# One multiply moved to ScalarE and one group of transposes moved behind two matmul groups, in a recurrent-attention and SwiGLU kernel

## The chip, the core and the metric

The kernel runs on one core of one Trainium2 chip. The metric is the device time of one execution in microseconds (us), lower is better. The core has five engines with instruction queues of their own: TensorE (PE in the profile; its weight loads are shown as PEld), VectorE (DVE), ScalarE (ACT), GpSimd (POOL) and SyncE (SP), which here issues most of the DMAs. Each queue runs in its own order, and engines wait for each other by semaphores.

## The reference

Two stages. The first is a linear recurrence per batch and head, with a state of 48 x 48, a decay w per key column and a bonus u for the current token. The second is a normalised SwiGLU network over its output.

```python
r, k, v, w: (4, 8, 768, 48)   u: (8, 48)
for t in range(S):
    cur = einsum('bhd,bhe->bhde', u * k[t], v[t])
    y[t] = einsum('bhd,bhde->bhe', r[t], state + cur)
    state = w[t][..., None] * state + einsum('bhd,bhe->bhde', k[t], v[t])
x = y as (3072, 384)
xn = x / sqrt(mean(x * x) + 1e-6) * rms_g
g = xn @ w_gate                       # (384, 1536)
out = (g * sigmoid(g) * (xn @ w_val)) @ w_out
```

## The kernel before

**Tiling.** The 768 tokens are cut into six superblocks n of 128 tokens. A superblock has four units n.j, one for each batch j: 128 tokens on the partitions and 384 columns (8 heads of 48). The recurrence is computed by chunks: the logarithms of w are summed up along the tokens by a matmul with a triangle of ones (cs_mm, L394 to L419), r is multiplied by the exponential of that sum and k by that of its negative (r_mul, L454; k_mul, L460). Then r and k are transposed, the scores of each head are computed (q_mm, L494), masked, and multiplied with v (y_mm, L541); older tokens come in through the state (st_mm, st_new). The bonus is added as a column by token (bonus_mul, bonus_sum, bonus_v). k_mul is done by VectorE in superblocks 0 and 1 and by GpSimd in the others.

**Transposes of r and k.** In superblocks 0 and 1 they are matmuls with an identity, eight for a unit: four of r, then four of k (rk_pe, L483), into one bank of PSUM, which ScalarE copies out (rk_tr, L492). From superblock 2 on they are DMAs.

**The network.** x of a unit is scaled by its root mean square on ScalarE (xn_mul, L584) and transposed into x^T, a tile xnt of 128 partitions x 3 groups c x 512 tokens of the superblock. In superblocks 0 to 3 TensorE does it (xn_pe), and VectorE multiplies by rms_g while it copies out (xn_out). In superblocks 4 and 5 four DMA transposes do it (xn_tr, L589), and then three instructions n.c multiply the groups c of x^T by rms_g in place (xn_gain, L611, each 128 x 512). Then come twelve column groups f: gate_mm and val_mm (L622, three matmuls each, one for each group c in the order 0, 1, 2), silu on ScalarE (L635, shown under the helper's line L234), h_mul on VectorE (L640). After all twelve, o_mm (L654) multiplies by w_out, twelve matmuls for each batch, o_out copies and out_dma stores.

**Order.** The order of every queue is written out by hand in the string ORDER: a list of steps "function.n.j", issued one after the other. An engine's queue is the part of this list that concerns the engine. Work of neighbouring superblocks is mixed: while the network of superblock n runs, the recurrence of n + 1 is computed. Steps "warm" are idle matmuls at the start.

**Banks.** PSUM is dealt out in three rings: "a" of two banks (ps_au, ps_av: gate results and sums), "b" of two (ps_bu, ps_bv: value results and sums) and "q" of four (ps_qu, ps_qv, ps_qx, ps_qz: all the rest). A step takes the bank of its ring that has been free the longest in the order of the list (psum, L221), so moving a step can change banks. In this change no step gets another bank or follows another user in it. Of interest below: val_mm.0.0 and then val_mm.0.3 use ps_bu, gate_mm.0.0 and gate_mm.0.2 use ps_au, gate_mm.0.3 and gate_mm.0.1 use ps_av, and gate_mm.4.0 and gate_mm.4.3 use ps_av.

**Tables.** ScalarE computes exponentials and logarithms under one function table and silu under another; `act` loads the other table when it changes (L232). Copies with a scale go past `act` and ask for no table.

The pieces of the order around the two edits, as they were:

```python
... exp_k.1.2 rk_tr.1.0 k_mul.1.3 gate_mm.0.0
rk_pe.1.1 val_mm.0.2 st_new.0.1 gate_mm.0.3 bonus_sum.1.0 silu.0.0 load_gv.1.1 val_mm.0.0 gate_mm.0.2 silu.0.3 silu.0.2
bonus_sum.1.1 rk_tr.1.1 h_mul.0.0 h_mul.0.2 r_mul.1.3 gate_mm.0.1 val_mm.0.3 gate_mm.0.9 ...
...
exp_r.5.2 cs_mm.5.0 o_mm.3.3 cs_add.5.0 exp_r.5.0 exp_k.5.2 out_dma.2.1 exp_k.5.0 bonus_v.5.3 r_mul.5.2 out_dma.3.2
r_mul.5.0 cs_mm.5.3 bonus_mul.5.2 o_mm.3.0 cs_add.5.3 load_v.5.2 k_mul.5.1 exp_k.5.3 xn_gain.4.1 xn_gain.4.0
bonus_mul.5.1 xn_gain.4.2 exp_r.5.3 r_mul.5.3 gate_mm.4.0 rk_tr.5.1 val_mm.4.1 silu.4.0 k_mul.5.0 gate_mm.4.1 ...
```

Of the kernel before, what the change touches and what calls it, by code (L numbers as in the profile page):

```python
# [11 lines left out]
AF = mybir.ActivationFunctionType  # L12
# [28 lines left out]
x_rstd.0.2 st_new.0.0 warm.35.0 r_mul.1.1 warm.11.0 cs_mm.1.3 x_sq.0.3 warm.28.0 xn_pe.0.0 xn_out.0.1 xn_out.0.0  # L41
warm.0.0 st_new.0.3 xn_mul.0.2 x_rstd.0.3 exp_k.1.3 xn_mul.0.3 xn_pe.0.2 cs_mm.1.2 xn_out.0.2 xn_pe.0.3 xn_out.0.3
st_mm.0.2 rk_pe.1.0 st_mm.0.1 k_mul.1.1 exp_r.1.3 exp_r.1.2 st_new.0.2 exp_k.1.2 rk_tr.1.0 k_mul.1.3 gate_mm.0.0
rk_pe.1.1 val_mm.0.2 st_new.0.1 gate_mm.0.3 bonus_sum.1.0 silu.0.0 load_gv.1.1 val_mm.0.0 gate_mm.0.2 silu.0.3 silu.0.2
bonus_sum.1.1 rk_tr.1.1 h_mul.0.0 h_mul.0.2 r_mul.1.3 gate_mm.0.1 val_mm.0.3 gate_mm.0.9 silu.0.1 bonus_mul.1.3
val_mm.0.1 h_mul.0.3 silu.0.9 gate_mm.0.6 q_mm.1.0 bonus_sum.1.3 silu.0.6 gate_mm.0.7 q_copy_o.1.1 q_copy_o.1.0
q_mask_o.1.0 q_mask_o.1.1 gate_mm.0.5 rk_pe.1.3 bonus_v.1.0 h_mul.0.1 silu.0.7 val_mm.0.7 load_r.2.2 q_mask_e.1.0
# [56 lines left out]
st_mm.4.2 h_mul.3.5 val_mm.3.11 silu.3.11 bonus_mul.5.0 x_add.4.3 ln.5.1 x_sq.4.2 st_mm.4.3 h_mul.3.11 cs_mm.5.1  # L104
x_sq.4.3 x_rstd.4.2 xn_mul.4.2 cs_add.5.1 load_r.5.1 ln.5.3 xn_tr.4.0 o_mm.3.2 x_rstd.4.3 o_out.3.2 xn_tr.4.1 xn_tr.4.2
exp_r.5.1 xn_mul.4.3 ln.5.2 o_mm.3.1 ln.5.0 cs_mm.5.2 exp_k.5.1 r_mul.5.1 xn_tr.4.3 st_new.4.3 cs_add.5.2 out_dma.2.3
exp_r.5.2 cs_mm.5.0 o_mm.3.3 cs_add.5.0 exp_r.5.0 exp_k.5.2 out_dma.2.1 exp_k.5.0 bonus_v.5.3 r_mul.5.2 out_dma.3.2
r_mul.5.0 cs_mm.5.3 bonus_mul.5.2 o_mm.3.0 cs_add.5.3 load_v.5.2 k_mul.5.1 exp_k.5.3 xn_gain.4.1 xn_gain.4.0
bonus_mul.5.1 xn_gain.4.2 exp_r.5.3 r_mul.5.3 gate_mm.4.0 rk_tr.5.1 val_mm.4.1 silu.4.0 k_mul.5.0 gate_mm.4.1 rk_tr.5.0
k_mul.5.3 val_mm.4.0 k_mul.5.2 bonus_sum.5.0 silu.4.1 st_new.4.2 cast_v.5.2 cast_v.5.3 bonus_sum.5.1 gate_mm.4.3  # L110
o_out.3.1 gate_mm.4.2 h_mul.4.1 load_v.5.0 o_out.3.3 bonus_sum.5.2 silu.4.3 o_out.3.0 silu.4.2 val_mm.4.2 h_mul.4.2
# [20 lines left out]
def kernel(  # L132
# [13 lines left out]
    nc = tc.nc  # L146
# [7 lines left out]
    KC = DM // 128  # L154
# [3 lines left out]
    TS = SB * L  # L158
# [15 lines left out]
    def sel(s):  # L174
        return {(int(x[0]), int(x[1])) for x in s.split()}
# [10 lines left out]
    RK_PE = sel("00 01 02 03 10 11 12 13")  # L186
    RK_DVE = sel("")
    GAIN_POOL = sel("")
    RPAIR = ()
    ODD_DVE = sel("00 01 02 03")  # L190
    RSTD_ACT = sel("00 01 02 03")
# [4 lines left out]
    def banks_of(fn, n, j):  # L196
        if fn == "q_mm":
            return [(x, n, c) for c in ((j, j + 1) if (n, j) in Q_PAIR else (j,)) for x in ("qe", "qo")]
        found = {
            "cs_mm": ("cs_r",) if n in ONE_SUM else ("cs_r", "cs_k"), "cs_add": ("cs_k", "cs_r"),  # L200
            "exp_r": ("cs_r",), "exp_k": ("cs_k",),
            "w_tot": () if (n, j) in EXPR_SB else ("cs_r",), "r_mul": () if (n, j) in EXPR_SB else ("cs_r",),
            "k_mul": () if (n, j) in EXPK_SB else ("cs_k",),
            "rk_pe": ("tr",), "rk_tr": ("tr",) if (n, j) in RK_PE else (),
            "q_mask_e": ("qe",), "q_copy_o": ("qo",), "q_mask_o": ("qo",) if (n, j) in ODD_DVE else (),
            "st_mm": ("st",), "st_new": ("st",), "y_mm": ("y",), "x_add": ("y",), "x_pe": ("y",),
            "x_sq": ("y",) if (n, j) in X_PE else (), "xn_mul": ("y",) if (n, j) in X_PE else (),
            "xn_pe": ("xt",), "xn_out": ("xt",), "gate_mm": ("g",), "silu": ("g",),
            "val_mm": ("v",), "h_mul": ("v",), "o_mm": ("o",), "o_out": ("o",), "warm": ("warm",),
        }  # L210
        return [(x, n, j) for x in found.get(fn, ())]

# [2 lines left out]
    for i, step in enumerate(steps):  # L215
        for key in banks_of(*step):
            last_use[key] = i
# [3 lines left out]
    def psum(ring, key, shape, dtype=FP32):  # L221
        slots = rings[ring]
        k = min((x for x in range(len(slots)) if slots[x][0] < at[0]), key=lambda x: slots[x])
        taken[0] += 1
        slots[k] = [last_use.get(key, -1), taken[0]]
        return psP.tile(shape, dtype, name="ps_" + ring + "uvxz"[k])
# [46 lines left out]
    gT = small.tile([128, KC], FP32)  # L273
# [9 lines left out]
    for i in range(EARLY):  # L283
# [6 lines left out]
        out=mask_lt, in_=mask_lt, compare_op=ALU.is_ge, fill=1.0,  # L290
# [26 lines left out]
        out=mw, in_=mw, compare_op=ALU.is_ge, fill=1.0,  # L317
# [24 lines left out]
    wg_sb = [persist.tile([128, KC, (b - a) * 128], BF16, name="wg_sb%d" % a) for a, b in zip(GV, GV[1:])]  # L342
    wv_sb = [persist.tile([128, KC, (b - a) * 128], BF16, name="wv_sb%d" % a) for a, b in zip(GV, GV[1:])]
# [21 lines left out]
    xnt, ht = {}, {}  # L365
    bank = {}
# [196 lines left out]
    def x_sq(n, j):  # L563
        c = j % 2 if n in RPAIR else 0
        if (n, j) not in rstd:
            rstd[n, j] = small.tile([128, 2, 2], FP32, name="rstd", bufs=4)
            if n in RPAIR:
                rstd[n, j - j % 2] = rstd[n, j - j % 2 + 1] = rstd[n, j]
        nc.scalar.activation(out=junk, in_=xb[n, j], func=AF.Square, accum_out=rstd[n, j][:, 0, c:c + 1])

    def x_rstd(n, j):
        w = 2 if n in RPAIR else 1
        ss, rs = rstd[n, j][:, 0, 0:w], rstd[n, j][:, 1, 0:w]
        if (n, j) in RSTD_ACT:
            act(LN_EXP, out=ss, in_=ss, func=AF.Ln, scale=1.0 / DM, bias=eps_col)
            act(LN_EXP, out=rs, in_=ss, func=AF.Exp, scale=-0.5)
        else:
            nc.gpsimd.tensor_scalar(out=ss, in0=ss, scalar1=1.0 / DM, scalar2=eps, op0=ALU.mult, op1=ALU.add)
            nc.gpsimd.tensor_tensor(out=rs, in0=ss, in1=mhalf[:, 0:w], op=ALU.pow)  # L579

    def xn_mul(n, j):
        xn = bank["xn", n, j] = pt.tile([128, DM], BF16, name="xn", bufs=3)
        c = j % 2 if n in RPAIR else 0
        nc.scalar.activation(out=xn, in_=xb[n, j], func=AF.Copy, scale=rstd[n, j][:, 1, c:c + 1])  # L584
# [22 lines left out]
                                    in1=gT.to_broadcast([128, KC, L]), op=ALU.mult)  # L607

    def xn_gain(n, c):
        eng = nc.gpsimd if (n, c) in GAIN_POOL else nc.vector  # L610
        eng.tensor_scalar(out=xnt[n][:, c, :], in0=xnt[n][:, c, :], scalar1=gT[:, c:c + 1],  # L611
                                scalar2=None, op0=ALU.mult)


    def units(ws, c, f):
        g = max(i for i, x in enumerate(GV) if x <= f)
        a = (f // FG * FG - GV[g]) * 128
        return ws[g][:, c, a:a + FG * 128].rearrange("p (m i) -> p i m", i=FG)[:, f % FG, :]

    def fc_mm(ps, ws, n, f):  # L620
        for c in range(KC):
            nc.tensor.matmul(ps, lhsT=units(ws, c, f), rhs=xnt[n][:, c, :],  # L622
                             start=(c == 0), stop=(c == KC - 1))

    def gate_mm(n, f):
        bank["g", n, f] = psum("a", ("g", n, f), [128, TS])
        fc_mm(bank["g", n, f], wg_sb, n, f)

    def val_mm(n, f):
        bank["v", n, f] = psum("b", ("v", n, f), [128, TS])  # L630
        fc_mm(bank["v", n, f], wv_sb, n, f)

    def silu(n, f):
        sg = bank["sg", n, f] = pt.tile([128, TS], BF16, name="sg", bufs=NSG)
# [38 lines left out]
    for step in ORDER.split():  # L673
        fn, n, j = step.split(".")
# [32 lines left out]
```

## Time and profile before

| | |
|---|---|
| median of 3 runs | 202.21 us (202.11 to 202.51) |
| profiled execution | 201.95 us, of which the span of instructions is 200.2 us |
| TensorE busy | 191.2 us, 95% of the span, 1557 matmuls |
| VectorE busy | 152.5 us, 76% |
| ScalarE busy | 136.3 us, 68%, with 10 table loads of 1.28 us |
| GpSimd busy | 125.6 us, 63% |
| DMA | 32.41 MB, mean 162 GB/s |

How the views are read: a timeline line has the start in us, the duration in us, the engine, the line of the kernel, the operation, output <- inputs, the shape and the count; several like instructions in a row are merged into one line, whose duration is that of the whole row. In brackets stands the idle time before it and what ended it. Matmuls are pipelined, so one starts before the other's modelled end: what counts for TensorE's queue is the distance from start to start. "Landed" is the time at which a DMA's data had arrived.

### The profile page before, as it was taken

What the parts mean: (1) busy time and instruction counts of PE and PEld (TensorE: products, weight loads), DVE (VectorE), ACT (ScalarE), POOL (GpSimd) and SP (SyncE); (2) the same over time, 40 slices, a digit from 0 to 9 for tenths busy, and PEclk for the clock granted to TensorE, in tenths of its full rate; (3) what the DMA queues carried; (4) which work ended last, traced back from release to release, by engine and by line L of the source; (5) the groups of instructions that cost most, each with busy time, mean ns of one, the idle gap of its engine ahead of it and who ended that gap; (6) DMA issues with size and microseconds to landing.
All of it is one profiled execution on the core that took longest, in us unless ns stands there. A gap on an engine that the chain in (4) does not pass through costs nothing.

```text
span 200.2 us, 4388 instructions
## 1 busy us (share of the span) xinstructions
PE 191.2 (95%) x1557; PEld 113.6 (57%) x1577; DVE 152.5 (76%) x291; ACT 136.3 (68%) x278; POOL 125.6 (63%) x184
## 2 busy tenths in 40 slices
PE   7987998999999999999999999999989999999994
PEld 3544665565665566665556665556645565555562
DVE  6357889889998799986999998887998773335611
ACT  3488987798968669967659958499766764164300
POOL 5358896097849987689978998976981852000000
PEclk9999999999999999999999999999999999999999
DMA  6999999999989999979999969993596112041012
GB/s 159 251 233 181 189 221 214 171 195 195 203 172 239 196 175 240 244 163 216 199 190 231 223 147 203 195 183 72 160 165 165 39 25 58 1 157 43 0 59 100
DMA packets 121566, 32.41 MB, mean 162 GB/s; under 512 B 116420, under 2 KB 120392, under 8 KB 121544
## 3 DMA queue, kind: packets, MB, share of 16 engines
q1 hardware_dynamic: 119504, 28.58, 67.6%
q0 software_dynamic: 2032, 3.54, 9.8%
q8 instruction: 12, 0.20, 0.4%
q14 instruction: 10, 0.08, 0.1%
q10 hardware_dynamic: 8, 0.00, 0.0%
HBM read 25.96 MB, written 4.72 MB: 153 GB/s over the span
## 4 chain that ended last, share of the span: by engine, by line
PE 83%; SPq 6%; DVE 5%; DMA 2%; issue 2%; ACT 1%; DVEq 0%
PE ps_bu L622 12%; PE ps_av L622 12%; PE ps_bv L622 12%; PE ps_au L622 11%; PE ps_qz L654 6%; PE ps_qv L654 5%; PE ps_qx L654 5%; PE ps_qu L654 5%; SPq L247 4%; DMA kt<-in_k_dram 2%; SPq L260 2%; DVE xnt L611 1%; DVE rk L460 1%; PE ps_qx L501 1%; PE ps_qu L501 1%
## 5 line engine op out<-in xcount | busy, mean ns | idle before, releaser
L654 PEld LDWEIGHTS <-ht 128*128 128x128 bf16 x300 | 28.4, 98 | 16.7
L234 ACT ACTIVATE sg<-ps_av 128x512 bf16<-128x512 f32 x37 | 22.2, 600 | 22.5 <-PE ps_av L622 14.0
L622 PEld LDWEIGHTS <-wg_sb 128*128 128x128 bf16 x216 | 23.0, 114 | 19.4 <-DVE xnt L611 0.7
L622 PEld LDWEIGHTS <-wv_sb 128*128 128x128 bf16 x216 | 22.8, 114 | 18.6 <-issue 0.6
L622 PE MATMUL ps_av<-xnt,wg_sb 128*128 128x512 bf16 x106 | 29.7, 380 | 1.1 <-DVE xnt L611 0.9
L466 POOL TENSOR_TENSOR ruk<-rt,kt 128x384 f32<-128x384 f32 x24 | 24.4, 1015 | 9.2 <-DMA rt<-in_r_dram 5.0
L640 DVE TENSOR_TENSOR ht<-ps_bv,sg 128x512 bf16<-128x512 f32 x36 | 24.7, 686 | 6.3 <-PE ps_bv L622 5.7
L640 DVE TENSOR_TENSOR ht<-ps_bu,sg 128x512 bf16<-128x512 f32 x36 | 24.8, 688 | 6.2 <-PE ps_bu L622 4.2
L622 PE MATMUL ps_bv<-xnt,wv_sb 128*128 128x512 bf16 x107 | 29.2, 379 | 0.1
L622 PE MATMUL ps_bu<-xnt,wv_sb 128*128 128x512 bf16 x100 | 28.6, 380 | 0.5
L622 PE MATMUL ps_au<-xnt,wg_sb 128*128 128x512 bf16 x99 | 27.8, 380 | 0.3
L234 ACT ACTIVATE sg<-ps_au 128x512 bf16<-128x512 f32 x35 | 20.9, 597 | 9.4 <-PE ps_au L622 8.1
L467 POOL TENSOR_TENSOR ruk<-ruk,u_bc 128x384 f32<-128x384 f32 x24 | 24.2, 1009 | 1.9
L519 POOL TENSOR_SCALAR_AFFINE_SELECT qts<-qts 128x512 bf16<-128x512 bf16 x20 | 13.1, 663 | 13.9 <-ACT qts L512 13.9
L476 POOL TENSOR_TENSOR ydiag<-vt,diag 128x384 f32<-128x384 f32 x24 | 20.1, 842 | 1.1 <-DVE diag L471 1.1
L460 POOL TENSOR_TENSOR rk<-kt,ek 128x384 bf16<-128x384 f32 x16 | 15.9, 1008 | 0.9 <-ACT ek L234 0.8
L234 ACT ACTIVATE lw<-wt 128x384 bf16<-128x384 f32 (+1 forms) x20 | 11.3, 581 | 4.7 <-DMA wt<-in_w_dram 4.7
L232 ACT ACT_TABLE_LOAD x10 | 12.8, 1283 | 1.8 <-PEq L691 1.7
L654 PE MATMUL ps_qz<-wo_sb,ht 128*128 128x384 bf16 (+1 forms) x84 | 13.8, 314 | 0.0
L471 DVE TENSOR_REDUCE diag<-ruk 128x8 f32<-128x384 f32 x24 | 13.0, 544 | 0.7 <-POOL ruk L467 0.7
L584 ACT ACTIVATE xn<-xb,rstd 128x384 bf16<-128x384 f32 x20 | 11.8, 609 | 1.2 <-POOL rstd L579 1.2
L654 PE MATMUL ps_qu<-wo_sb,ht 128*128 128x384 bf16 x72 | 12.7, 326 | 0.0
(179 smaller groups left out, 377.5 us busy)
## 6 DMA issues: line engine op xcount, KB each, us to landing
rt<-in_r_dram SPq DMA_DIRECT2D x24, 192.0 KB, 4.0
kt<-in_k_dram SPq DMA_DIRECT2D x24, 192.0 KB, 3.9
vt<-in_v_dram SPq DMA_DIRECT2D x24, 192.0 KB, 3.8
out_dram<-ob SPq DMA_DIRECT2D x23, 192.0 KB, 2.4
wt<-in_w_dram SPq DMA_DIRECT2D x16, 192.0 KB, 3.8
wt<-in_w_dram SPq DMA_DIRECT2D x4, 384.0 KB, 4.6
wo_sb<-in_moe_w_out_dram POOLq DMA_DIRECT2D x3, 384.0 KB, 6.4
wg_sb<-in_moe_w_gate_dram POOLq DMA_DIRECT2D x1, 768.0 KB, 10.1
```

What stands on the lines that cost most here:

```text
L232: nc.scalar.preload_act_table_set(table_name)
L234: return nc.scalar.activation(**kw).ins
L460: eng.tensor_tensor(out=rk[:, n % 2, j, 1, :, 0:D], in0=inp["k", n, j], in1=bank["cs_k", n, j][:, 0:DM].rearrange("p (h d) -> p h d", h=H) ...
L466: nc.gpsimd.tensor_tensor(out=ruk[n, j], in0=inp["r", n, j], in1=inp["k", n, j], op=ALU.mult)
L467: nc.gpsimd.tensor_tensor(out=ruk[n, j], in0=ruk[n, j], in1=u_bc, op=ALU.mult)
L471: nc.vector.tensor_reduce(out=diag[n, j].rearrange("p h o -> p (h o)"), in_=ruk[n, j], axis=mybir.AxisListType.X, op=ALU.add)
L476: nc.gpsimd.tensor_tensor(out=ydiag[n, j], in0=inp["v", n, j], in1=diag[n, j].to_broadcast([128, H, D]), op=ALU.mult)
L519: nc.gpsimd.affine_select(out=qts[n, j][:, 1], in_=qts[n, j][:, 1], compare_op=ALU.is_gt, fill=0.0, base=0, pattern=[[0, NP], [1, 128]], c ...
L584: nc.scalar.activation(out=xn, in_=xb[n, j], func=AF.Copy, scale=rstd[n, j][:, 1, c:c + 1])
L622: nc.tensor.matmul(ps, lhsT=units(ws, c, f), rhs=xnt[n][:, c, :], start=(c == 0), stop=(c == KC - 1))
L640: nc.vector.tensor_tensor(out=ht[n][:, f, :], in0=bank.pop(("v", n, f)), in1=bank.pop(("sg", n, f)), op=ALU.mult)
L654: nc.tensor.matmul(ps[:, cols], lhsT=ht[n][:, f, b * L:(b + 1) * L], rhs=wo_sb[:, f, cols], start=(f == 0), stop=(f == FC - 1))
```

## The change

Two steps move. The transposes of unit 1.1 (rk_pe.1.1) are issued after val_mm.0.2 and gate_mm.0.3 instead of ahead of them. The multiply of group c = 1 of x^T of superblock 4 (xn_gain.4.1) becomes an activation of ScalarE, a copy with a scale by partition, and stands on ScalarE between exp_k.5.0 and exp_k.5.3; the multiplies of the groups 0 and 2 stay on VectorE. Besides, gate_mm and val_mm get a form in two halves (gate_h, val_h) that no step of the order uses; without it they issue the same matmuls as before.

```diff
-rk_pe.1.1 val_mm.0.2 st_new.0.1 gate_mm.0.3 bonus_sum.1.0 silu.0.0 load_gv.1.1 val_mm.0.0 gate_mm.0.2 silu.0.3 silu.0.2
+val_mm.0.2 st_new.0.1 gate_mm.0.3 rk_pe.1.1 bonus_sum.1.0 silu.0.0 load_gv.1.1 val_mm.0.0 gate_mm.0.2 silu.0.3 silu.0.2
...
-exp_r.5.2 cs_mm.5.0 o_mm.3.3 cs_add.5.0 exp_r.5.0 exp_k.5.2 out_dma.2.1 exp_k.5.0 bonus_v.5.3 r_mul.5.2 out_dma.3.2
-r_mul.5.0 cs_mm.5.3 bonus_mul.5.2 o_mm.3.0 cs_add.5.3 load_v.5.2 k_mul.5.1 exp_k.5.3 xn_gain.4.1 xn_gain.4.0
+exp_r.5.2 cs_mm.5.0 o_mm.3.3 cs_add.5.0 exp_r.5.0 exp_k.5.2 out_dma.2.1 exp_k.5.0 xn_gain.4.1 bonus_v.5.3 r_mul.5.2
+out_dma.3.2 r_mul.5.0 cs_mm.5.3 bonus_mul.5.2 o_mm.3.0 cs_add.5.3 load_v.5.2 k_mul.5.1 exp_k.5.3 xn_gain.4.0
...
+    GAIN_ACT = sel("41")
...
     def xn_gain(n, c):
+        if (n, c) in GAIN_ACT:
+            nc.scalar.activation(out=xnt[n][:, c, :], in_=xnt[n][:, c, :], func=AF.Copy, scale=gT[:, c:c + 1])
+            return
         eng = nc.gpsimd if (n, c) in GAIN_POOL else nc.vector
...
-    def fc_mm(ps, ws, n, f):
+    def fc_mm(ps, ws, n, f, cols, first):
         for c in range(KC):
-            nc.tensor.matmul(ps, lhsT=units(ws, c, f), rhs=xnt[n][:, c, :],
-                             start=(c == 0), stop=(c == KC - 1))
+            nc.tensor.matmul(ps[:, cols], lhsT=units(ws, c, f), rhs=xnt[n][:, c, cols],
+                             start=(first and c == 0), stop=(c == KC - 1))
...
     def gate_mm(n, f):
+        if ("g", n, f) in bank:
+            fc_mm(bank["g", n, f], wg_sb, n, f, slice(TS // 2, TS), False)
+            return
         bank["g", n, f] = psum("a", ("g", n, f), [128, TS])
-        fc_mm(bank["g", n, f], wg_sb, n, f)
+        fc_mm(bank["g", n, f], wg_sb, n, f, slice(0, TS), True)
```

More of the change, by code (lines that the diff above doesn't have):

```diff
@@ L207, in banks_of @@
             "x_sq": ("y",) if (n, j) in X_PE else (), "xn_mul": ("y",) if (n, j) in X_PE else (),
-            "xn_pe": ("xt",), "xn_out": ("xt",), "gate_mm": ("g",), "silu": ("g",),
-            "val_mm": ("v",), "h_mul": ("v",), "o_mm": ("o",), "o_out": ("o",), "warm": ("warm",),
+            "xn_pe": ("xt",), "xn_out": ("xt",), "gate_mm": ("g",), "gate_h": ("g",), "silu": ("g",),
+            "val_mm": ("v",), "val_h": ("v",), "h_mul": ("v",), "o_mm": ("o",), "o_out": ("o",), "warm": ("warm",),
         }
@@ L618, in units, with gate_h, val_h @@
         return ws[g][:, c, a:a + FG * 128].rearrange("p (m i) -> p i m", i=FG)[:, f % FG, :]
-    def fc_mm(ps, ws, n, f):
+    def fc_mm(ps, ws, n, f, cols, first):
         for c in range(KC):
-            nc.tensor.matmul(ps, lhsT=units(ws, c, f), rhs=xnt[n][:, c, :],
-                             start=(c == 0), stop=(c == KC - 1))
+            nc.tensor.matmul(ps[:, cols], lhsT=units(ws, c, f), rhs=xnt[n][:, c, cols],
+                             start=(first and c == 0), stop=(c == KC - 1))
+    def gate_h(n, f):
+        bank["g", n, f] = psum("a", ("g", n, f), [128, TS])
+        fc_mm(bank["g", n, f], wg_sb, n, f, slice(0, TS // 2), True)
+    def val_h(n, f):
+        bank["v", n, f] = psum("b", ("v", n, f), [128, TS])
+        fc_mm(bank["v", n, f], wv_sb, n, f, slice(0, TS // 2), True)
     def gate_mm(n, f):
+        if ("g", n, f) in bank:
+            fc_mm(bank["g", n, f], wg_sb, n, f, slice(TS // 2, TS), False)
+            return
         bank["g", n, f] = psum("a", ("g", n, f), [128, TS])
-        fc_mm(bank["g", n, f], wg_sb, n, f)
+        fc_mm(bank["g", n, f], wg_sb, n, f, slice(0, TS), True)
     def val_mm(n, f):
+        if ("v", n, f) in bank:
+            fc_mm(bank["v", n, f], wv_sb, n, f, slice(TS // 2, TS), False)
+            return
         bank["v", n, f] = psum("b", ("v", n, f), [128, TS])
-        fc_mm(bank["v", n, f], wv_sb, n, f)
+        fc_mm(bank["v", n, f], wv_sb, n, f, slice(0, TS), True)
     def silu(n, f):
```

## The prediction

> **What bounds the kernel now.** I read the chain of work that ended last first, then the table of who waited for whom, then the timelines of each engine around the two places that the change touches.
>
> Of the page, part 2 (the granted clock) and part 4 (the chain):
>
> ```profile
> PEclk9999999999999999999999999999999999999999
> ...
> PE 83%; SPq 6%; DVE 5%; DMA 2%; issue 2%; ACT 1%; DVEq 0%
> ```
>
> 83% of the span's chain is TensorE's own work at full clock, so an edit pays only where it removes a stall of TensorE or shortens TensorE's own queue. From 30.7 us on, TensorE's stalls of over 0.1 us are three in number: one ended by L460 at 32.39, two ended by L611 at 146.94 and 147.94. Everywhere else its matmuls follow each other. The change touches just these places.
>
> **Place A, 31 to 36 us: the transposes of unit 1.1.** TensorE's timeline from 31.3 to 32.7:
>
> ```profile
> 31.10 0.38 PE L622 MATMUL ps_au<-xnt,wg_sb 128*128 128x512 bf16 x1
> 31.32 0.39 PE L483 MATMUL ps_qv<-ident,rk 128*128 128x128 bf16 x4
> 32.39 0.40 PE L483 MATMUL ps_qv<-ident,rk 128*128 128x128 bf16 x4 [0.69 <-DVE rk L460]
> 32.62 0.38 PE L622 MATMUL ps_bv<-xnt,wv_sb 128*128 128x512 bf16 x1
> ```
>
> The reader is to see that the four transposes of r start at once and the four of k wait. Four transposes hold TensorE for 0.23 us (32.39 to 32.62), so without the wait the k ones would start near 31.54: the stall costs 32.39 - 31.54 = 0.85 us of TensorE's queue (0.69 is the idle that is left after the modelled ends of its matmuls).
>
> VectorE's timeline from 31 to 36 says what else stands there:
>
> ```profile
> 30.44 1.89 DVE L460 TENSOR_TENSOR rk<-kt,ek 128x384 bf16<-128x384 f32 x1
> 32.26 0.55 DVE L536 TENSOR_TENSOR st<-ps_qz,wcol 128x384 bf16<-128x384 f32 x1
> 32.72 0.89 DVE L460 TENSOR_TENSOR rk<-kt,ek 128x384 bf16<-128x384 f32 x1
> 33.54 0.55 DVE L536 TENSOR_TENSOR st<-ps_qu,wcol 128x384 bf16<-128x384 f32 x1
> 34.00 1.00 DVE L471 TENSOR_REDUCE diag<-ruk 128x8 f32<-128x384 f32 x2
> 34.92 0.68 DVE L640 TENSOR_TENSOR ht<-ps_bu,sg 128x512 bf16<-128x512 f32 x1
> ```
>
> VectorE runs without a gap from 30.44 to 35.60, and nothing in its queue changes. Replay TensorE's queue with the new order, a group of three L622 matmuls at 0.65 us (three starts 0.216 apart) and eight transposes at 0.45: val_mm.0.2 starts at 31.32, gate_mm.0.3 at 31.97, the transposes at 32.61 (k_mul.1.1 ended at 32.33, so no wait), val_mm.0.0 at 33.06, gate_mm.0.2 at 33.71, gate_mm.0.1 at 34.36, val_mm.0.3 at 35.01 instead of 35.86. What the two groups moved ahead need is there: val_mm.0.2's weights landed at 29.56, and ScalarE had read the two banks by 29.11 and 29.90. But val_mm.0.3 writes ps_bu, the bank of val_mm.0.0, and h_mul.0.0 reads it until 34.92 + 0.68 = 35.60. With the 0.06 us that TensorE takes to start after VectorE (146.88 to 146.94 below), val_mm.0.3 can start at 35.66: **0.65 of the 0.85 us comes back as a new wait for L640, and 0.20 us is left.**
>
> The transposes now end near 33.2 instead of 32.8, but rk_tr.1.1 on ScalarE stands behind silu.0.2, which ended at 36.01 before and at about 35.2 now; they have 2 us of cover there. Gate banks: silu.0.0 ends at 33.44 and gate_mm.0.2 needs it at 33.71; silu.0.3 ends near 33.95 and gate_mm.0.1 needs it at 34.36. Both hold.
>
> After 35.66 VectorE leads TensorE again. Whether the 0.20 reaches 146 us depends on every later release. The closest that I found, laying TensorE's starts beside the ends of what frees their banks, are r_mul.4.3 and w_tot.4.3 (end 119.22, next matmul in that bank 119.50) and st_new.4.0 (end 121.68, next in that bank 121.95). Both margins are 0.27 to 0.28, less 0.06 of start-up, so 0.20 just fits even if VectorE would not move at all. I take 0.20, with the ends 0 and 0.85.
>
> **Place B, 144 to 149 us: the gain of superblock 4.** VectorE's timeline, cut to 145.5 to 147.75 (earlier and later pieces are merged into one line):
>
> ```profile
> 145.23 2.66 DVE L611 TENSOR_SCALAR xnt<-xnt,gT 128x512 bf16<-128x512 bf16 x3
> ```
>
> TensorE's, 146.7 to 148.3:
>
> ```profile
> 146.94 0.41 PE L622 MATMUL ps_av<-xnt,wg_sb 128*128 128x512 bf16 x1 [0.34 <-DVE xnt L611]
> 147.94 0.38 PE L622 MATMUL ps_av<-xnt,wg_sb 128*128 128x512 bf16 x1 [0.59 <-DVE xnt L611]
> 148.15 0.38 PE L622 MATMUL ps_bv<-xnt,wv_sb 128*128 128x512 bf16 x1
> ```
>
> The three multiplies run in the order 4.1, 4.0, 4.2: narrower windows give 145.23 to 145.88, 145.80 to 146.88, and 146.80 to 147.88. gate_mm.4.0 needs 4.0 first and 4.2 last. The last o_mm of superblock 3 started its twelfth matmul at 146.27, so gate_mm.4.0 could start at 146.43 and val_mm.4.1 at 147.08; it started at 148.15. The stall is 1.07 us.
>
> Why 1.08 us each? In superblock 5 (171 us, GpSimd idle) the same instruction takes 0.35. GpSimd's timeline, 145.1 to 147.85:
>
> ```profile
> 144.74 1.00 POOL L467 TENSOR_TENSOR ruk<-ruk,u_bc 128x384 f32<-128x384 f32 x1
> 145.69 3.05 POOL L460 TENSOR_TENSOR rk<-kt,ek 128x384 bf16<-128x384 f32 x3
> ```
>
> GpSimd's instructions end at 145.73, 146.73 and 147.73, and each multiply ends 0.15 after one of them: a multiply is let through once per GpSimd instruction. The Trainium skill (SBUF — State Buffer, "SBUF: two separate sides") says that VectorE's fast modes and GpSimd hold one port pair in turn, an exclusive lock for the whole instruction; by it, as by the rows, the first multiply left would end at 145.88 and the second at 146.88. The trace agrees.
>
> With 4.1 gone from VectorE, 4.0 takes the slot that ended at 145.88 and 4.2 the one that ended at 146.88. Then gate_mm.4.0 starts at 146.43, its third matmul at 146.94 (146.86 without any wait) and val_mm.4.1 at 147.15: **1.00 us saved.**
>
> The cost on ScalarE. Its timeline, 144.5 to 146.3:
>
> ```profile
> 144.23 0.49 ACT L234 ACTIVATE ek<-ps_bv 128x384 f32<-128x384 f32 x1
> 145.35 0.49 ACT L234 ACTIVATE ek<-ps_bu 128x384 f32<-128x384 f32 x1 [0.63 <-DVE ps_bu L424]
> 145.74 0.49 ACT L234 ACTIVATE ps_au<-ps_au 128x384 f32<-128x384 f32 x1
> 146.24 1.28 ACT L232 ACT_TABLE_LOAD   x1
> ```
>
> The new instruction stands in the idle 0.63 us, between exp_k.5.0 and exp_k.5.3. The trace has no such copy of 128x512; the nearest row is xn_mul (L584, 128x384, same function and a scale by partition), 0.61 us, and 128 more columns add 0.13 by the exps (0.47) and the silus (0.60). I estimate 0.74 us, the bounds are 0.60 and 0.85. Started at about 144.62 (activations overlap by 0.1) it ends at 145.36, and exp_k.5.3 moves by 0.1 at most. Its input is there: the last transpose landed at 143.33. If the cover were gone, 0.74 us on ScalarE would push the table load's end from 147.53 to 148.27 and silu.4.0 to 148.87; gate_mm.4.3 needs that bank at 149.10 (three groups of 0.65 after 147.15), so it still costs nothing. The Trainium skill speaks against the move (ScalarE: Activation LUTs, "Rules for kernel authors": a multiply belongs on VectorE, up to about three times faster there in bf16). The rows give 0.35 against an estimated 0.74, but beside GpSimd 1.08, and ScalarE idles.
>
> From 147 us on, weights, values and transposes of superblock 5 have landed long before use, and its own multiplies end at 171.93 where TensorE needs them at 173.88, or 172.7 with the gain: no new wait. The end of the kernel is TensorE's queue, then o_out and its store, unchanged. The new functions gate_h and val_h are not in the order, so they issue nothing.
>
> **Sum.** The profiled execution took 201.95 us (span 200.2 and 1.75 around it): -0.20 - 1.00 = -1.2 gives a span of 199.0 and 200.75. The median of the runs shown is 0.26 above the profiled execution, 202.21; so 201.0.
>
> **Rivals.**
> 1. Only B reaches the end: the 0.20 of A is given back at one of the transitions where VectorE has no gaps (119 to 122 us). 201.2.
> 2. B's slot is missed: the two multiplies left fall one GpSimd instruction later, 4.2 ends again at 147.88, and TensorE still resumes at 148.15; only A's 0.20 is left, 202.0. For it: the lockstep above is set by GpSimd, not by VectorE. Against it: cs_add.5.3 ahead of them still ends at 145.32, before the slot that ends at 145.73. The Trainium skill's lock (same page and section), taken by who starts first, would give this if GpSimd's next instruction came ahead of VectorE's.
> 3. A keeps all of its 0.85, were h_mul.0.0 earlier: 200.4. Against it: VectorE's unbroken row.
> 4. Slower: the copy on ScalarE brings table loads with it, two of 1.28 us. ScalarE is then late by 0.74 + 2.57 - 0.63 = 2.7 us, silu.4.0 ends at 150.8, gate_mm.4.3 waits for its bank until 150.9 instead of 149.1: 1.8 lost against 1.2 won, 202.8. It ends slower than before from 2.1 us of lateness on (0.9 of cover and the 1.2 won). Against it: L584 runs the same function 24 times amid ten loads that all stand before a change between logarithm or exponential and silu.
>
> **How the numbers follow.** Forecast 201.0 (200.7 to 201.3): 0.58. Rival 1 and partial losses up to 201.6: 0.20. Rival 2: 0.12. Rival 3: 0.03. Rival 4 and the like: 0.07. The range 200.4 to 202.0 leaves out rival 4 and the edges. A measurement of this kernel can tell about 0.2% (0.4 us) from no change: faster 0.81, same 0.12, slower 0.07.
>
> **What would show it.** Right: no wait for L460 at 32; a wait of about 0.6 for L640 at 35.7 on ps_bu; two L611 between 145 and 147 and one activation of about 0.74 in ScalarE's gap; TensorE's wait for L611 under 0.1; a span near 199.0. Wrong: val_mm.0.3 at 35.0 (A was worth more), a matmul of gate_mm.4.0 still starting 0.5 us late (B missed its slot), an eleventh table load, or new TensorE stalls between 36 and 145.

## The result and the profile after

The changed kernel takes 201.06 us (median of 8 runs, 200.29 to 201.61) beside 202.18 for the kernel before on the same chip: a ratio of 0.9936, 95% interval 0.9916 to 0.9956, so 1.1 us or 0.6% faster. Forecast were 201.0 and 1.2. Its profiled execution, the slowest of the eight, took 201.61 us with a span of 199.9, though, only 0.3 less than the span before, and not the 199.0 of the sum. Both facts have to be explained.

The page of the changed kernel, the granted clock and the chain of work that ended last (line 622 is now 626, 640 is 658, 654 is 672, 460 is 461, 611 is 612 on ScalarE and 615 on VectorE):

```profile
PEclk9999999999999999999999999999999999999999
...
PE 77%; SPq 6%; DMA 6%; DVE 5%; POOL 3%; issue 1%; ACT 0%; DVEq 0%
```

DMA's share of the chain rose from 2 to 6%: something new stands in TensorE's way, which comes below.

**Place A.** TensorE's timeline of the changed kernel, 31.2 to 37:

```profile
31.12 0.81 PE L626 MATMUL ps_au<-xnt,wg_sb 128*128 128x512 bf16 x3
31.77 0.81 PE L626 MATMUL ps_bv<-xnt,wv_sb 128*128 128x512 bf16 x3
32.42 0.81 PE L626 MATMUL ps_av<-xnt,wg_sb 128*128 128x512 bf16 x3
33.06 0.61 PE L484 MATMUL ps_qv<-ident,rk 128*128 128x128 bf16 x8
...
34.81 0.81 PE L626 MATMUL ps_av<-xnt,wg_sb 128*128 128x512 bf16 x3
36.09 0.81 PE L626 MATMUL ps_bu<-xnt,wv_sb 128*128 128x512 bf16 x3 [0.47 <-DVE ht L658]
36.74 0.59 PE L626 MATMUL ps_au<-xnt,wg_sb 128*128 128x512 bf16 x2
```

The eight transposes run as one row, without a wait. But val_mm.0.3 starts 1.28 us after gate_mm.0.1 instead of 0.65: 0.64 us of waiting for L658, the h_mul. From gate_mm.0.0 to gate_mm.0.9 it is 36.74 - 31.12 = 5.62 us, and was 36.51 - 30.67 = 5.84. VectorE's timeline beside it, 33.9 to 36.9:

```profile
33.98 0.54 DVE L537 TENSOR_TENSOR st<-ps_qu,wcol 128x384 bf16<-128x384 f32 x1
34.45 0.99 DVE L472 TENSOR_REDUCE diag<-ruk 128x8 f32<-128x384 f32 x2
35.36 0.67 DVE L658 TENSOR_TENSOR ht<-ps_bu,sg 128x512 bf16<-128x512 f32 x1
```

No idle is shown: h_mul.0.0 waits for nothing but its turn behind the two reductions, ends at 36.04, and TensorE goes on at 36.09.

**Place B.** TensorE (146.9 to 148), VectorE (145.5 to 147.6), GpSimd (145.2 to 147.5) and ScalarE (144.8 to 148) of the changed kernel:

```profile
147.12 0.88 PE L626 MATMUL ps_av<-xnt,wg_sb 128*128 128x512 bf16 x3
147.84 0.38 PE L626 MATMUL ps_bv<-xnt,wv_sb 128*128 128x512 bf16 x1
```

```profile
145.44 0.57 DVE L425 TENSOR_TENSOR ps_bu<-ps_au,lw 128x384 f32<-128x384 f32 x1 [0.22 <-ACT ek L235]
145.92 1.65 DVE L615 TENSOR_SCALAR xnt<-xnt,gT 128x512 bf16<-128x512 bf16 x2
147.49 0.54 DVE L455 TENSOR_TENSOR rk<-rt,ps_au 128x384 bf16<-128x384 f32 x1
```

```profile
145.42 1.00 POOL L468 TENSOR_TENSOR ruk<-ruk,u_bc 128x384 f32<-128x384 f32 x1
146.38 2.05 POOL L461 TENSOR_TENSOR rk<-kt,ek 128x384 bf16<-128x384 f32 x2
```

```profile
144.92 0.50 ACT L235 ACTIVATE ek<-ps_bv 128x384 f32<-128x384 f32 x1
145.29 0.73 ACT L612 ACTIVATE xnt<-xnt,gT 128x512 bf16<-128x512 bf16 x1
146.04 0.49 ACT L235 ACTIVATE ek<-ps_bu 128x384 f32<-128x384 f32 x1
```

gate_mm.4.0 now starts where the last o_mm leaves TensorE, its three matmuls run together, and val_mm.4.1 follows 0.72 us after its first. The two multiplies left take the slots forecast: they end at 146.57 and 147.57, 0.15 after GpSimd's instructions (146.42, 147.42). The copy takes 0.73 us and ScalarE is at its next exponential 0.02 after that. From the first matmul of o_mm.3.0 to val_mm.4.1 it is 147.84 - 145.17 = 2.67 us, before 148.15 - 144.48 = 3.67.

**The new stall.** TensorE's timeline, 52.4 to 54.6, in o_mm.0.0:

```profile
52.45 1.46 PE L672 MATMUL ps_qx<-wo_sb,ht 128*128 128x384 bf16 x8
54.35 0.48 PE L672 MATMUL ps_qx<-wo_sb,ht 128*128 128x384 bf16 x2 [0.44 <-DMA wo_sb<-in_moe_w_out_dram]
```

After eight of twelve matmuls the last third of w_out has not landed: the ninth would start at 53.74 and starts at 54.35, 0.61 us lost. It was issued at 47.08 and landed at 54.31, 7.2 us later; before it took 6.4 (46.87 to 53.30) and beat its use, 53.52, by 0.22.

**The account of the two profiled executions.** Each is a head (until gate_mm.0.0's first matmul), a stretch (to o_mm.5.0's first) and a tail (10.96 us in the changed kernel, 10.97 before). The head was 31.12 us instead of 30.67, +0.45. In the stretch: A -0.22, B -1.00, w_out +0.61, and -0.15 at 59 us, where in the profile before cs_mm.2.3 waited that long for r_mul.2.1 to leave its bank: 157.82 instead of 158.58. (Four of the twelve profiles here have such a wait there, of 0.15 to 0.36 us, with the change and without. TensorE's timelines name other releasers for it or show no idle time, but in each of the four cs_mm.2.3 starts 0.15 us after r_mul.2.1 ends.) Together -0.3 in the span. The forecast terms are there in full; the head and w_out hide most of them in this one execution.

### The profile page after: what moved, and what is told of

It reads as the page before. It is cut to its first block, busy times and chain, and to the rows that moved or that the text cites. A ratio compares the mean times of both kernels' runs of the same rounds, so it can differ in the third digit from the quotient of the medians.

```text
span 199.9 us, 4406 instructions
## 1 busy us (share of the span) xinstructions
PE 192.6 (96%) x1577; PEld 113.7 (57%) x1577; DVE 151.6 (76%) x290; ACT 136.9 (69%) x279; POOL 125.5 (63%) x184
## 4 chain that ended last, share of the span: by engine, by line
PE 77%; SPq 6%; DMA 6%; DVE 5%; POOL 3%; issue 1%; ACT 0%; DVEq 0%
PE ps_av L626 10%; PE ps_bu L626 10%; PE ps_bv L626 10%; PE ps_au L626 10%; PE ps_qz L672 6%; PE ps_qu L672 6%; PE ps_qv L672 5%; PE ps_qx L672 5%; SPq L248 4%; DMA wo_sb<-in_moe_w_out_dram 4%; DMA kt<-in_k_dram 2%; SPq L261 2%; DVE rk L461 2%; POOL qts L520 1%; PE ps_bv L557 1%
## 5 line engine op out<-in xcount | busy, mean ns | idle before, releaser
L626 PE MATMUL ps_bu<-xnt,wv_sb 128*128 128x512 bf16 x108 | 29.3, 380 | 0.5 <-DVE ht L658 0.5
L658 DVE TENSOR_TENSOR ht<-ps_bu,sg 128x512 bf16<-128x512 f32 x36 | 24.7, 687 | 6.2 <-PE ps_bu L626 4.2
L658 DVE TENSOR_TENSOR ht<-ps_bv,sg 128x512 bf16<-128x512 f32 x36 | 24.7, 685 | 6.1 <-PE ps_bv L626 5.7
L626 PE MATMUL ps_au<-xnt,wg_sb 128*128 128x512 bf16 x105 | 28.5, 380 | 0.0
L672 PE MATMUL ps_qx<-wo_sb,ht 128*128 128x384 bf16 x72 | 12.8, 326 | 0.4 <-DMA wo_sb<-in_moe_w_out_dram 0.4
```

Of the source, the lines that this page charges most:

```text
L626: nc.tensor.matmul(ps[:, cols], lhsT=units(ws, c, f), rhs=xnt[n][:, c, cols], start=(first and c == 0), stop=(c == KC - 1))
L658: nc.vector.tensor_tensor(out=ht[n][:, f, :], in0=bank.pop(("v", n, f)), in1=bank.pop(("sg", n, f)), op=ALU.mult)
L672: nc.tensor.matmul(ps[:, cols], lhsT=ht[n][:, f, b * L:(b + 1) * L], rhs=wo_sb[:, f, cols], start=(f == 0), stop=(f == FC - 1))
```

## The experiments

Times are compared with runs of the kernel before on the same chip. The time is the median of the runs and the ratio that of their means, so the two can differ a little. Since the head alone differs by 1.1 us from profile to profile (30.14 to 31.24), and both edits lie behind it, I read the mechanisms from distances inside the trace: **A** from gate_mm.0.0's first matmul to gate_mm.0.9's, **B** from o_mm.3.0's to val_mm.4.1's, and the **stretch** as above. (The expectations give a stretch to val_mm.5.11, which is 0.87 us shorter than this one. Where a trace has no record of val_mm.4.1's first matmul, it is put 0.215 us ahead of the second.)

| kernel | time, us (before) | ratio, 95% interval | A | B | stretch |
|---|---|---|---|---|---|
| before | 202.21 | | 5.84 | 3.67 | 158.58 |
| changed | 201.06 (202.18) | 0.9936, 0.9916 to 0.9956 | 5.62 | 2.67 | 157.82 |
| changed, again | 200.92 (201.95) | 0.9944, 0.9921 to 0.9966 | 5.61 | 2.65 | 157.19 |
| only the transposes | 201.75 (201.86) | 0.9994, 0.9975 to 1.0014 | 5.62 | 3.66 | 158.21 |
| only the multiply | 200.80 (201.86) | 0.9947, 0.9926 to 0.9967 | 5.84 | 2.67 | 157.42 |
| reductions moved | 200.20 (201.86) | 0.9918, 0.9889 to 0.9948 | 4.98 | 2.66 | 156.60 |
| reductions moved, again | 200.33 (202.08) | 0.9899, 0.9865 to 0.9933 | 4.98 | 2.67 | 156.99 |
| w_out earlier | 200.73 (201.86) | 0.9945, 0.9926 to 0.9964 | 5.62 | 2.65 | 157.20 |
| reductions and w_out | 200.13 (202.08) | 0.9902, 0.9866 to 0.9939 | 4.98 | 2.67 | 156.83 |
| two multiplies on ScalarE | 200.37 (201.95) | 0.9918, 0.9893 to 0.9944 | 5.73 | 2.60 | 157.50 |
| reductions and two multiplies | 200.39 (201.95) | 0.9937, 0.9900 to 0.9974 | 4.98 | 2.60 | 156.77 |
| k_mul of superblock 5 left out | 201.0, one run (201.95) | | 5.83 | 2.60 | 157.35 |

**Only the transposes.** The kernel before with the first line of the order changed.

```diff
-rk_pe.1.1 val_mm.0.2 st_new.0.1 gate_mm.0.3 bonus_sum.1.0 ...
+val_mm.0.2 st_new.0.1 gate_mm.0.3 rk_pe.1.1 bonus_sum.1.0 ...
```

> The kernel before with only the transposes of unit 1.1 moved. My theory: from the first matmul of gate_mm.0.0 to the first of gate_mm.0.9 TensorE takes 5.61 us as in the changed kernel (5.84 before), with a wait of about 0.6 for L640 ahead of val_mm.0.3, and those 0.23 us are then given back at 54 us, where o_mm.0.0 needs the last third of w_out, whose landing is not tied to TensorE: time within 0.2 us of before. Rival: nothing else holds it, and the time is 0.2 us below before. Second rival: A is worth 0.5 or more.

A is 5.6, with the wait for L640 of 0.64. But my theory of where it goes fell: no wait for w_out shows at 54 us, and the gain is still there at the end of the stretch (-0.37, of which 0.15 is the accident of the profile before). w_out landed at 53.27 and was needed at 53.47. Its request had moved too: load_wo stands on GpSimd behind masks that wait for q_mm.1.0, and so goes out earlier when TensorE is earlier (counted from gate_mm.0.0's first matmul, 15.96 us here instead of 16.20, and 15.43 with the reductions moved). The time is 0.1 below, and its interval (0.5 below to 0.3 above) holds both 0 and 0.2.

**Only the multiply.** The changed kernel with that line as it was.

> The changed kernel with the transposes of unit 1.1 back in their old place, so that only the multiply on ScalarE is left. My theory: from the first matmul of o_mm.3.0 to the first of val_mm.4.1 TensorE takes 2.67 us instead of 3.67, nothing gives it back, and the time is 1.0 us below before, 0.9 to 1.2. Rival (both parts count in full): 1.0 below before and 0.2 above the changed kernel.

B is 2.67 and the time 1.06 us below. The stretch falls by 1.16, that is 1.00 and the 0.15 of the profile before. The times do not tell this kernel from the changed one (1.12 and 1.03 us below before): that A's 0.2 counts is read from the stretch alone.

**The reductions behind h_mul.0.0.** What takes A's rest?

```diff
-val_mm.0.2 st_new.0.1 gate_mm.0.3 rk_pe.1.1 bonus_sum.1.0 silu.0.0 ...
-bonus_sum.1.1 rk_tr.1.1 h_mul.0.0 h_mul.0.2 r_mul.1.3 ...
+val_mm.0.2 st_new.0.1 gate_mm.0.3 rk_pe.1.1 silu.0.0 ...
+rk_tr.1.1 h_mul.0.0 bonus_sum.1.0 bonus_sum.1.1 h_mul.0.2 r_mul.1.3 ...
```

> The changed kernel with the two reductions bonus_sum.1.0 and 1.1 moved behind h_mul.0.0 on VectorE. If h_mul.0.0 on VectorE is what took 0.65 of the 0.85 us back, the stretch from gate_mm.0.0 to gate_mm.0.9 falls from 5.61 to about 4.97 us and the wait ahead of val_mm.0.3 goes. If something else held val_mm.0.3, the stretch stays at 5.6. If the landing of w_out's last third holds TensorE at 54 us, the time of the whole does not fall with it: 0 to 0.3 us below the changed kernel, and a wait for w_out of 0.6 us or more shows; if it does not hold, 0.6 us below.

VectorE's timeline of this kernel, 33.8 to 37, and TensorE's, 31.2 to 37:

```profile
33.83 0.55 DVE L537 TENSOR_TENSOR st<-ps_qu,wcol 128x384 bf16<-128x384 f32 x1
34.29 0.68 DVE L658 TENSOR_TENSOR ht<-ps_bu,sg 128x512 bf16<-128x512 f32 x1
34.89 1.00 DVE L472 TENSOR_REDUCE diag<-ruk 128x8 f32<-128x384 f32 x2
35.81 0.68 DVE L658 TENSOR_TENSOR ht<-ps_bv,sg 128x512 bf16<-128x512 f32 x1
```

```profile
34.64 0.81 PE L626 MATMUL ps_av<-xnt,wg_sb 128*128 128x512 bf16 x3
35.29 0.81 PE L626 MATMUL ps_bu<-xnt,wv_sb 128*128 128x512 bf16 x3
35.94 0.81 PE L626 MATMUL ps_au<-xnt,wg_sb 128*128 128x512 bf16 x3
```

h_mul.0.0 starts as soon as its input is there, val_mm.0.3 follows gate_mm.0.1 after 0.65 us, A is 4.98. So it was the turn behind the two reductions that gave 0.64 of the 0.85 back. The stretch is 156.60, 0.59 below the shorter of the changed kernel's two, and the time 1.66 us below before, 0.5 more than the changed kernel won: the rest of A is real and reaches the end. w_out holds nothing up here either, though barely: it lands at 52.88 and its use is at 52.94.

**The request for w_out.** One step moved in the order, the last third of w_out right behind the second:

```diff
-load_wo.1.0 silu.0.5 ...
+load_wo.1.0 load_wo.2.0 silu.0.5 ...
...
-q_mm.1.2 bonus_mul.1.2 load_wo.2.0 cast_v.1.3 ...
+q_mm.1.2 bonus_mul.1.2 cast_v.1.3 ...
```

> The changed kernel with the last third of w_out asked for right behind the second, about 44.3 instead of 47.1 us. If its landing held TensorE at 54 us in the profile of the changed kernel (0.6 us there), that wait is gone and the time is 0.1 to 0.6 us below the changed kernel. If that wait was an accident of one execution, no change within 0.1 us. If the earlier request delays the loads of superblock 2 beside it, slower by 0.2 or more, with a wait for a load in the profile.

No wait for w_out (landed at 52.20), and the time is 1.13 below before, as much as the changed kernel: no change. The earlier request bought little: counted from gate_mm.0.0 it goes out at 13.12 us instead of 15.96, but takes 8.8 us to land and is there at 21.89, instead of 23.19 and 22.57 in the two profiles of the changed kernel.

**The changed kernel again.**

> The changed kernel once more, unchanged. If the wait of 0.6 us for w_out's last third at 54 us in its first profile was an accident of that execution, the last third lands about 6.4 us after its issue as in the other profiles, no such wait shows, and the stretch from the first matmul of gate_mm.0.0 to the first of val_mm.5.11 is about 156.4 us instead of 156.95. If the change brings it about, the wait shows again.

No wait for w_out; it took 6.6 us to land (47.18 to 53.80) and beat its use by 0.06. The stretch is 157.19, 0.63 shorter than in the first profile. So the 0.61 us was that execution's: of the ten profiles with the request in its old place, the landing takes 6.4 to 6.8 us in nine and 7.2 in that one. There the first two thirds were slow as well (7.1 and 8.6 us, 5.8 to 6.5 and 7.5 to 7.8 in the other nine); why is open. The margin is small enough that it shows again in one other profile, below.

**Two multiplies on ScalarE.** Only group 0 stays on VectorE.

```diff
-    GAIN_ACT = sel("41")
+    GAIN_ACT = sel("41 42")
...
-... exp_k.5.0 xn_gain.4.1 bonus_v.5.3 r_mul.5.2
+... exp_k.5.0 xn_gain.4.1 xn_gain.4.2 bonus_v.5.3 r_mul.5.2
...
-bonus_mul.5.1 xn_gain.4.2 exp_r.5.3 ...
+bonus_mul.5.1 exp_r.5.3 ...
```

> The changed kernel with a second multiply, of group 2, on ScalarE behind that of group 1, so that only group 0 stays on VectorE. ScalarE is then about 0.6 us late for exp_k.5.3, exp_r.5.3 and the table load. My theory: that lateness is covered (0.9 us until gate_mm.4.3 wants silu.4.0's bank), and the stretch from o_mm.3.0 to val_mm.4.1 falls from 2.67 to 2.60 us; the time is within 0.2 us of the changed kernel. Rival (ScalarE has no cover): TensorE waits 0.5 us or more for silu.4.0 or exp_r.5.3 between 147 and 151 us, and the time is 0.4 or more above the changed kernel.

ScalarE's timeline of this kernel, 144 to 149:

```profile
144.56 1.34 ACT L612 ACTIVATE xnt<-xnt,gT 128x512 bf16<-128x512 bf16 x2
145.79 0.50 ACT L235 ACTIVATE ek<-ps_bu 128x384 f32<-128x384 f32 x1
146.16 0.51 ACT L235 ACTIVATE ps_au<-ps_au 128x384 f32<-128x384 f32 x1
146.69 1.28 ACT L233 ACT_TABLE_LOAD   x1
147.98 0.60 ACT L235 ACTIVATE sg<-ps_av 128x512 bf16<-128x512 f32 x1
```

exp_k.5.3 starts 1.23 us after the first copy; in the changed kernel it was 0.75 (145.29 to 146.04). ScalarE is half a microsecond late, the first silu comes right behind the table load, and TensorE has no stall from 146 to 151. B is 2.60, the full 1.07 won. The stretch, 157.50, is nevertheless longer than the changed kernel's 157.19, by two things ahead of the edit: A is 5.73 here, and cs_mm.2.3 waits 0.23. The time is 0.5 below the changed kernel on the same chip, but the two intervals overlap, and no distance in the trace gives more than 0.07: I don't count it as a gain.

**Was it GpSimd that made the multiplies slow?** The kernel before, in which the four k_mul of superblock 5 are left out. Their products are then missing from superblock 5, so the kernel serves only for its distances.

```diff
     def k_mul(n, j):
+        if n == 5:
+            return
```

> The kernel before without the four multiplies of k in superblock 5 (k_mul.5.0 to 5.3 are left out, so GpSimd is free of them at 145 to 149 us). If VectorE's multiplies of superblock 4 took 1.08 us because GpSimd held the port, those that no longer stand beside a GpSimd instruction take about 0.35 us, all three on VectorE end by about 146.5, and the stretch from o_mm.3.0 to val_mm.4.1 falls from 3.67 to 2.7 us or less without ScalarE. If they are slow for another reason (their in-place form, TensorE or DMA reading the tile), they still take about 1 us each and the stretch stays at 3.6.

VectorE's and GpSimd's timelines of this kernel (144.5 to 149, the first lines of it, and 144.5 to 147, the whole answer; line 611 is 613 here, 467 is 469):

```profile
145.38 0.87 DVE L613 TENSOR_SCALAR xnt<-xnt,gT 128x512 bf16<-128x512 bf16 x3
146.41 0.56 DVE L454 TENSOR_TENSOR rk<-rt,ps_au 128x384 bf16<-128x384 f32 x1 [0.16 <-ACT ps_au L234]
```

```profile
143.91 1.00 POOL L469 TENSOR_TENSOR ruk<-ruk,u_bc 128x384 f32<-128x384 f32 x1
```

All three multiplies take 0.35 us and are done 0.87 us after the first starts, instead of 2.66. B is 2.60 without ScalarE's help. Nothing else about the multiplies was touched, so GpSimd's instructions beside them were the cause of the 1.08 us.

**Together.** The reductions moved and two multiplies on ScalarE:

> The reductions behind h_mul.0.0 and two multiplies on ScalarE together. The parts add up: 0.86 from the first place, 1.07 from the second, so 1.9 us below before in the stretch from gate_mm.0.0 to val_mm.5.11 and about 1.6 to 2.0 in the time; no stall of TensorE over 0.1 us from 31 us on. If one part spoils the other, less than 1.4.

The distances add up (A 4.98, B 2.60), but w_out lands 6.8 us after its request, 53.29, and o_mm.0.0 loses 0.27 to it; the stretch is 1.81 below before, the time 1.56 by the medians and 1.3 by the means (interval 0.5 to 2.0). The 1.6 to 2.0 without a stall that I expected did not come. Last, the reductions with the earlier w_out, and the reductions again beside it:

> The kernel with the reductions behind h_mul.0.0, and w_out's last third asked for right behind the second. If its landing is the next bound of this version (the profiles so far had it land from 0.1 us ahead of its use to 0.3 us behind), it now lands some 0.7 us earlier, no wait shows at 53 us, and the time is 0 to 0.3 us below the version without it, 1.6 to 1.9 below the kernel before. If it only takes the loads beside it back, no change or slower.

> The kernel with the reductions behind h_mul.0.0 once more, unchanged, beside the version with the earlier request on the same chip: about 1.6 us below the kernel before (0.8%), a stretch of about 4.97 us from gate_mm.0.0 to gate_mm.0.9, and a wait for w_out at 53 us of 0 to 0.3 us. If the first measurement was luck, the time is near the changed kernel's, 1.1 below before.

200.13 and 200.33 us, 0.98 and 1.01% below before. The reductions' gain is confirmed; the earlier w_out lands at 51.40, 0.7 ahead of its use, and takes the risk of that wait away, but what it is worth can't be told from these runs. In both profiles the wait of cs_mm.2.3 at 58 to 59 us shows (0.23 and 0.36 against the first profile of the reductions). By the stretch the versions with the reductions behind h_mul.0.0 are the best tried: 156.6 to 157.0 beside 157.2 and more. The times say it less sharply. The reductions alone or with the earlier w_out are 0.8 to 1.0% below before and the changed kernel 0.6%, but the two multiplies alone are 0.8% below and the reductions with them 0.6%, and the intervals overlap.

## Why the prediction was right, step by step

- **The bound.** TensorE's queue, with three stalls after 31 us: right, but for a fourth of 0.15 us at 59 us, which the timeline does not show as idle time. Each change in A and B came through to the end of the stretch.
- **A, 0.20 us.** Measured 0.22 (5.84 to 5.62). The step that decided it, VectorE's unbroken row up to h_mul.0.0, was right: the wait came back as 0.64 us for h_mul, and moving the two reductions away released it. Rival 3 (A keeps 0.85) was false for this change and true as soon as they moved.
- **B, 1.00 us.** Measured 1.00 and 1.02 in the two profiles of the changed kernel and 1.00 in the kernel with the multiply alone. The slots by GpSimd's instructions came as forecast (Rival 2 did not occur), and the experiment without k_mul shows the cause. "1.08 us each" holds for the second and third of the row; the first took 0.65 (145.23 to 145.88), and the slots of the sum had that right. The Trainium skill's exclusive lock (SBUF — State Buffer, "SBUF: two separate sides") agrees with both: 1.08 beside GpSimd, 0.35 without it.
- **ScalarE, 0.74 us at no cost.** Measured 0.73, exp_k.5.3 not late (it starts 0.03 us after its input is there, 146.01), table loads still ten (Rival 4 did not occur). The cover that I claimed behind it, 0.9 us, was tested to half a microsecond. The Trainium skill's rule to keep multiplies on VectorE (ScalarE: Activation LUTs, "Rules for kernel authors") did not hold here, because VectorE took 1.08 us for it beside GpSimd and ScalarE was idle.
- **No new TensorE stall between 36 and 145.** This failed in the first profile after. The prediction laid TensorE's starts beside the ends of what frees their banks, and not beside the landing of w_out, whose margin of 0.22 us was smaller than the 0.27 that it called the closest. The stall was 0.61 us there, absent in the second profile. It also passed over cs_mm.2.3, which by the same method stood 0.15 after r_mul.2.1, with no margin at all in the profile before. So it did not hold that 0.20 just fits even if VectorE would not move. A came through because r_mul.2.1 is earlier in most executions: in seven of the twelve profiles cs_mm.2.3 starts 0.31 to 0.48 after it (0.36 with the transposes alone). In this step the forecast had luck.
- **The span of 199.0.** It was 199.9 and then 199.4. The sum was made against one execution and took its head for fixed; the head was 0.45 and 0.57 us longer in these two. The median of the runs, 201.06, is where the sum put it, and the runs nearest to it have spans of 199.3 and 199.4: 199.0 and the 0.26 that the prediction laid between the profiled execution and the median. That the two agree to 0.06 us is closer than the runs can tell: the interval of the ratio, 0.9916 to 0.9956, allows a gain of 0.9 to 1.7.

## What to carry to other kernels

A stall that is moved past is only worth what the next late thing leaves. So replay the queue in the new order, and for each later step lay its start beside everything that it waits for: the last reader of its bank, and the landing of the data that it loads. Before an instruction is moved to the engine where it is slower alone, look at what it takes in its place: one multiply beside GpSimd took three times its time on VectorE, and was quicker on ScalarE. And judge a gain of a microsecond by distances inside the trace and by many runs, not by the span of one profile, whose first 31 us alone varied by 1.1.

## What the runs showed of the hardware

- VectorE's bf16 multiply of 128x512 in SBUF by a scalar per partition takes 0.35 us with GpSimd idle. Beside a row of GpSimd's f32 products it takes 1.08 us (0.65 the first of a row) and ends 0.15 us after one of them, while these grow from 1.00 to 1.04 us only: here it was VectorE that waited.
- The same multiply as a copy with scale on ScalarE takes 0.73 us, 0.61 apart in a row.
- The landing of the same 384 KB of w_out from the same place in the order took 6.4 to 7.2 us from one execution to the next. Asked for 2.8 us earlier it took 8.7 to 8.8 us, so that only 0.7 to 1.3 us of the 2.8 were won.
